# Feed-forward pieces beside attention: 64x128 tiles of the array in place of pairs of 64x64

## The chip, the cores and the metric

The kernel runs on one core of a Trainium2 chip. The metric is the device time of one execution in microseconds (us). The median of three runs of the kernel before is 318.04 us (316.34 to 318.82). The execution that was profiled took 318.09 us.

## The reference

Attention with a softmax whose denominator has one more term, for 8 batches, 12 heads, 448 positions and a head size of 64, and behind it a feed-forward layer in which the largest of three products is taken, for 8 x 448 = 3,584 tokens of 768 values:

```python
def _attn_ref(q, k, v):
    scale = 1.0 / np.sqrt(q.shape[-1])
    scores = scale * np.matmul(q, k.transpose(0, 1, 3, 2))
    m = np.max(scores, axis=-1, keepdims=True)
    e = np.exp(scores - m)
    attn = e / (np.sum(e, axis=-1, keepdims=True) + np.exp(-m) + 1e-09)
    return np.matmul(attn, v)                     # (8, 12, 448, 64)

def _moe_ref(x, w1, w2, w3, w_out):               # w1, w2, w3, w_out: 768 x 768
    h = np.maximum(np.maximum(x @ w1, x @ w2), x @ w3)
    return h @ w_out
```

`x` is the attention's output with the heads side by side. The inputs and the output are float32.

## The kernel before, in words

The matmuls take 16-bit operands and sum in float32. The twelve heads of a batch are worked in three groups of four, so there are 24 groups, and a group's operands lie as two row halves of 64 partitions (`half(0)`, `half(1)`) by two columns, `c` = 0 and 1.

**Attention.** One visit (`visit`, L307) makes the scores of one block of 64 keys of a group with four matmuls on 64 rows by 64 columns of the TensorE array, one in each corner (`score_tile`, L291 to L301, tile `stp`; `TILES` gives the four corners). ACT takes the exponential (L318), DVE sums the blocks (L328). Per group there is one set of four matmuls for the denominator (`den_group`) and seven sets of four for the product with `v` (`num_group`), both through `av_tiles` (L340 to L348, matmuls at L342); ACT makes the reciprocal (L362, L369) and DVE the product that gives `xT` (`norm_group`, L397).

**Feed-forward beside attention.** A piece is one 128 x 448 block of an up product (`up_piece`: batch, column block `fc`, which of the three weights) or one 128 x 384 block of the output (`out_piece`). Each contracts 768 values, in `NDC` = 6 blocks of 128 rows, into one PSUM bank.

**Three phases.** In the first (to some 71 us in the trace) pieces run as ordinary matmuls on 128 rows by 128 columns (L534, L557) between the 64x64 matmuls of attention. In the second (71.7 to 237.4 us) attention of groups 7 to 23 goes on, and pieces run as *half steps*, which is what the change touches. In the third there is no attention, and the rest of the feed-forward runs on 128 by 128 (L1034, L1236).

**Half steps.** `piece_parts` (L741) gives the width (`S` = 448 or `NW` = 384 columns) and two functions that slice weights and moving data. `half_step(r)` (L768) does one of a piece's six blocks on row half `r`: it has to write 128 output rows, and does so with two matmuls, `c` = 0 and 1, of 64 rows by 64 columns (L782), into the lower and the upper 64 partitions of the piece's bank. Both row halves work on different pieces, since both write whole banks: each takes a batch of three pieces in another order (`turns`). A piece is done by one half first and then by the other, which starts with `start` unset and adds to what lies in the bank; before that an empty instruction on PE waits until the first half's last matmuls have ended (`wait_for`, L758, on `p["last"]`). When the second half is through, DVE or ACT empties the bank (`up_piece`, L518 to L523; `out_piece`, L565 to L575).

**Order.** The whole program is written out by hand: each engine works its list in that order, with semaphores between engines. `step()` (L830) gives a half step to row half 0 and then one to row half 1. The loop at L970 walks through groups and the entries of `ORDER` (seven visits, the denominator, the product with `v`), and puts steps between them, as many as the planner's rates ask for (`steps_for`) or as are needed until a score bank should be free (`for_pair`, from booked costs of DVE and ACT in units of steps). So stretches of half steps and sets of attention matmuls alternate on PE.

Of the kernel before, what the change touches and what calls it, by code (L numbers as in the profile page):

```python
# [14 lines left out]
ts = bass.ts  # L15
# [7 lines left out]
def kernel(  # L23
# [11 lines left out]
    nc = tc.nc  # L35
# [4 lines left out]
    KC = 64  # L40
    NJ = S // KC
    NDC = DM // 128
# [50 lines left out]
    def ring_bank(name):  # L93
        ring[0] += 1
        pool = single_pools[ring[0] // 2 % 2]
        return pool.tile([128, 512], FP32, tag="bank1", name=name)
# [7 lines left out]
    def half(n):  # L104
        return slice(n * KC, n * KC + KC)
# [54 lines left out]
    for _ in range(WQ):  # L160
        for r in range(2):
            for c in range(2):
                nc.tensor.matmul(
                    out=warm[r][c * KC : c * KC + KC, 0:WN],
                    lhsT=ones16[r * KC : r * KC + KC],
                    rhs=warm16[r * KC : r * KC + KC],
                    start=True,
                    stop=True,
# [3 lines left out]
    w_sb = [cpool.tile([128, NDC, DFF], MMDT, name=f"w{i}") for i in range(4)]  # L172
# [324 lines left out]
    hT = {}  # L497
    outs = {}

    def new_h(b, fc, i):  # L500
        if b // 2 not in hT:
            hT[b // 2] = ht_pool.tile([128, NFC, 2 * S], MMDT, tag="hT", name="hT")
# [158 lines left out]
    start = """  # L661
# [79 lines left out]
    def piece_parts(f, a):  # L741
        if f is up_piece:
            b, fc, i = a
            new_h(b, fc, i)
            return (
                S,
                lambda k, r, c: w_sb[i][half(r), k, fc * 128 + c * KC : fc * 128 + c * KC + KC],
                lambda k, r: xT[b][half(r), k],
            )
        bp, t, nh = a  # L750
        return (
            NW,
            lambda k, r, c: hT[bp][half(r), k, t * 128 + c * KC : t * 128 + c * KC + KC],
            lambda k, r: wout_sb[half(r), k, ts(nh, NW)],
        )


    def wait_for(matmuls):  # L758
        nop = nc.tensor.nop()
        for mm in matmuls:  # L760
            tc.add_manual_dep(
                nop.ins,
                mm.ins.name,
                mybir.DependencyInfo(mybir.DependencyClass.Sync, mybir.DependencyReason.DATA),
                reason="both row halves write one bank",
            )

    def half_step(r):  # L768
        n, k = divmod(count[r], NDC)
        count[r] += 1  # L770
        p = flow[turns[r][n]]
        if k == 0 and "parts" not in p:
            p["parts"] = piece_parts(p["f"], p["a"])
            p["bank"] = ring_bank("piece")
            p["first"] = r
        elif k == 0:
            wait_for(p["last"])
        w, lhs, rhs = p["parts"]
        p["last"] = []
        for c in range(2):  # L780
            p["last"].append(
                nc.tensor.matmul(  # L782
                    out=p["bank"][half(c), 0:w],
                    lhsT=lhs(k, r, c),
                    rhs=rhs(k, r),
                    start=(r == p["first"] and k == 0),
                    stop=(r != p["first"] and k == NDC - 1),
                )
            )
        if r != p["first"] and k == NDC - 1:  # L790
            p["f"](*p["a"], bank=p["bank"], done=True)
            p["done"] = True
# [37 lines left out]
    def step():  # L830
        if count[0] == NDC * len(turns[0]) and (len(pieces) >= 3 or last_batch[0] and pieces):
            m = len(flow)
            now = pieces[:3]
            del pieces[:3]
            flow.extend({"f": f, "a": a} for f, a, w in now)
            for r in range(2):
                turns[r] += [m + x for x in ((0, 2, 1), (1, 0, 2))[r] if x < len(now)]
        before = sum(count)
        idle = not ready(0)
        if not idle:  # L840
            half_step(0)
        if (count[1] + LAG < count[0] or idle) and ready(1):
            half_step(1)
        steps[0] += 1
        do_late()
        return sum(count) > before
# [123 lines left out]
    for i in range(MID, NI + 1):  # L970
        for op, j, w in ORDER if i > MID else ORDER[4:]:
# [23 lines left out]
            if op == "N":  # L995
# [4 lines left out]
                t = max(steps[0] + 1, state[i - 1]["recip"])  # L1000
# [253 lines left out]
    def in_turn(*units):  # L1254
        return [u[slot] for slot in range(max(map(len, units))) for u in units if slot < len(u)]
# [20 lines left out]
    first = in_turn(*(up(2, f) for f in range(SOONER, 3)))  # L1276
# [64 lines left out]
```

## Time and profile before

| what | us |
| --- | --- |
| median of three runs | 318.04 (316.34 to 318.82) |
| the profiled execution | 318.09 |
| its span, first to last instruction | 316.3 |
| PE busy in the span | 301.6 (95%) |
| PE weight loads busy | 216.3 (68%) |
| DVE busy | 246.0 (78%) |
| ACT busy | 230.8 (73%) |
| L782, piece matmuls of 448 and of 384 columns, busy | 121.7 and 29.4 |

Busy time of PE counts a stretch with at least one matmul in flight. A matmul's record is longer than the time after which the next can start, so the distance between starts tells the pace, and the duration doesn't. In the profile, `64*64` ahead of a shape is the part of the array that an instruction takes, rows by columns. The granted TensorE clock is given as a share of full speed.

### The profile page before, as it was taken

What the parts mean: (1) busy time and instruction counts of PE and PEld (TensorE: products, weight loads), DVE (VectorE), ACT (ScalarE), POOL (GpSimd) and SP (SyncE); (2) the same over time, 40 slices, a digit from 0 to 9 for tenths busy, and PEclk for the clock granted to TensorE, in tenths of its full rate; (3) what the DMA queues carried; (4) which work ended last, traced back from release to release, by engine and by line L of the source; (5) the groups of instructions that cost most, each with busy time, mean ns of one, the idle gap of its engine ahead of it and who ended that gap; (6) DMA issues with size and microseconds to landing.
All of it is one profiled execution on the core that took longest, in us unless ns stands there. A gap on an engine that the chain in (4) does not pass through costs nothing.

```text
span 316.3 us, 11901 instructions
## 1 busy us (share of the span) xinstructions
PE 301.6 (95%) x5200; PEld 216.3 (68%) x5200; DVE 246.0 (78%) x453; ACT 230.8 (73%) x315; POOL 82.8 (26%) x137
## 2 busy tenths in 40 slices
PE   6779999999999999999999999999999999999992
PEld 6557777658999767777679867777765555556551
DVE  3546598999889787988877898877867994989652
ACT  1999859987888987888887889999844547451540
POOL 8654341220433333434423434110000000000220
PEclk9999999999999999999999999999999999999998
DMA  8999999699778999789999999970003000002676
GB/s 149 192 203 205 208 208 204 89 149 179 118 104 135 180 171 182 99 124 168 229 136 137 100 172 232 155 89 4 2 2 101 4 0 2 0 0 72 186 236 205
DMA packets 59348, 40.58 MB, mean 128 GB/s; under 512 B 32256, under 2 KB 56288, under 8 KB 59296
## 3 DMA queue, kind: packets, MB, share of 16 engines
q0 software_dynamic: 25104, 21.80, 47.4%
q1 hardware_dynamic: 33648, 17.21, 27.7%
q8 instruction: 40, 0.66, 0.9%
q10 hardware_dynamic: 544, 0.82, 0.9%
q14 instruction: 12, 0.10, 0.1%
HBM read 42.47 MB, written 11.01 MB: 169 GB/s over the span
## 4 chain that ended last, share of the span: by engine, by line
PE 83%; ACT 8%; DVE 3%; issue 3%; DMA 1%; DVEq 0%; ACTq 0%
PE piece L782 35%; PE bank_a L1034 11%; PE stp L294 9%; PE av L342 8%; PE bank_s L1034 8%; PE p_i L534 4%; ACT eTp L416 3%; PE bank_a L1236 2%; PE piece L534 2%; ACT eT L318 2%; PE den L342 1%; DMA first_k<-in_k_dram 1%; PE piece L557 1%; DVE eS L328 1%; ACT rb L460 1%
## 5 line engine op out<-in xcount | busy, mean ns | idle before, releaser
L318 ACT ACTIVATE eT<-stp 128x896 f16<-128x896 f32 x147 | 129.1, 921 | 21.3 <-PE stp L294 21.1
L782 PE MATMUL piece<-xT,w 64*64 64x448 f16 x1968 | 121.7, 350 | 0.4 <-DVE xT L397 0.3
L782 PEld LDWEIGHTS <-w 64*64 64x64 f16 x1968 | 79.3, 107 | 17.0 <-issue 1.6
L294 PE MATMUL stp<-qkT 64*64 64x448 f16 (+2 forms) x756 | 65.2, 334 | 3.4 <-issue 1.3
L328 DVE TENSOR_TENSOR eS<-eS,eT 128x896 f16<-128x896 f16 x105 | 65.0, 619 | 3.4 <-ACT eT L318 0.2
L523 DVE TENSOR_TENSOR hT<-hT,piece 128x448 f16<-128x448 f16 x52 | 32.2, 619 | 13.9 <-PE piece L782 8.8
L294 PEld LDWEIGHTS <-qkT 64*64 64x64 f16 x756 | 29.4, 105 | 18.5 <-issue 7.3
L342 PE MATMUL av<-eT,ld_v 64*64 64x448 f16 x588 | 32.9, 350 | 0.2
L342 PEld LDWEIGHTS <-ld_v 64*64 64x64 f16 x756 | 26.5, 107 | 7.0 <-issue 1.5
L397 DVE TENSOR_TENSOR xT<-av,rb 128x448 f16<-128x448 f32 x42 | 24.2, 619 | 8.7 <-PE av L342 7.3
L114 POOL DMA_DIRECT2D ld_v<-in_v_dram x28 | 16.7, 598 | 52.5 <-PE stp L294 31.8
L782 PE MATMUL piece<-w,hT 64*64 64x384 f16 x456 | 29.4, 323 | 0.1
L583 POOL DMA_DIRECT2D out_dram<-o x7 | 3.8, 536 | 93.7 <-DVE o L1164 92.1
L114 POOL DMA_DIRECT2D ld_k<-in_k_dram x26 | 15.4, 595 | 39.5 <-PE stp L294 35.1
L362 ACT ACTIVATE rb<-den 128x896 f32<-128x896 f32 x21 | 19.3, 917 | 8.4 <-PE den L342 8.2
L416 ACT ACTIVATE eTp<-stp 128x768 f16<-128x768 f32 (+3 forms) x24 | 18.2, 821 | 7.1 <-PE stp L294 7.0
L534 PEld LDWEIGHTS <-w 128*128 128x128 f16 x216 | 18.9, 98 | 5.3 <-issue 3.6
L1034 PEld LDWEIGHTS <-comb 128*128 128x128 f16 x132 | 12.9, 98 | 12.2 <-issue 0.4
L782 PEld LDWEIGHTS <-hT 64*64 64x64 f16 x456 | 18.6, 107 | 3.6 <-issue 0.3
L369 ACT ACTIVATE rb<-rb 128x896 f32<-128x896 f32 x21 | 20.0, 952 | 0.2
L534 PE MATMUL p_i<-xT,w 128*128 128x192 f16 (+1 forms) x156 | 16.4, 257 | 0.6 <-DVE xT L490 0.6
L114 POOL DMA_DIRECT2D ld_q<-in_q_dram x26 | 15.7, 617 | 1.1 <-issue 1.1
(103 smaller groups left out, 405.0 us busy)
## 6 DMA issues: line engine op xcount, KB each, us to landing
out_dram<-o_sb SPq DMA_DIRECT2D x28, 192.0 KB, 4.9
ld_v<-in_v_dram POOLq DMA_DIRECT2D x28, 112.0 KB, 4.3
ld_k<-in_k_dram POOLq DMA_DIRECT2D x26, 112.0 KB, 3.5
ld_q<-in_q_dram POOLq DMA_DIRECT2D x26, 112.0 KB, 4.9
out_dram<-o SPq DMA_DIRECT2D x14, 192.0 KB, 3.3
ld_q<-in_q_dram POOLq DMA_DIRECT2D x11, 224.0 KB, 9.7
ld_k<-in_k_dram POOLq DMA_DIRECT2D x10, 224.0 KB, 9.5
ld_v<-in_v_dram POOLq DMA_DIRECT2D x10, 224.0 KB, 9.0
```

What stands on the lines that cost most here:

```text
L114: return eng.dma_start(out=dst[half(hp)].rearrange("p s j d -> p s (j d)"), in_=rows_of(name, i)[half(hp)])
L294: mm = nc.tensor.matmul(out=out[half(c), r], lhsT=qkT[half(r), 0, j, h], rhs=qkT[half(r), 1, q0:q1, h], start=True, stop=True,)
L318: nc.scalar.activation(out=st["eT"][:, j], in_=stp[:, :, 0:S], func=AF.Exp, scale=scale, bias=-math.log(EDIV))
L328: nc.vector.tensor_tensor(out=st["eS"], in0=st["eT"][:, 0] if j == 1 else st["eS"], in1=st["eT"][:, j], op=ALU.add,)
L342: nc.tensor.matmul(out=outs[r][half(c)], lhsT=weights(r, c), rhs=moving(r, c), start=start, stop=stop,)
L369: nc.scalar.activation(out=st["rb"], in_=st["rb"], func=AF.Exp, bias=math.log(LAMBDA), scale=-1.0)
L397: nc.vector.tensor_tensor(out=xT[b][:, 2 * g + r, :], in0=banks[r][:, 0:S], in1=state[i]["rb"][:, r], op=ALU.mult)
L416: nc.scalar.activation(out=eT[:, j0 : j0 + n].rearrange("p j r q -> p r j q"), in_=stp[:, :, 0 : n * nq].rearrange("p r (j q) -> p r j q", ...
L523: nc.vector.tensor_tensor(out=dst, in0=dst, in1=p_i[:, 0:S], op=ALU.max)
L534: nc.tensor.matmul(out=p_i[:, ts(j, nq)], lhsT=w_sb[i][:, dc, ts(2 * fp + j, 128)], rhs=xT[b][:, dc, q0 * KC : q1 * KC], start=(dc == 0), ...
L782: nc.tensor.matmul(out=p["bank"][half(c), 0:w], lhsT=lhs(k, r, c), rhs=rhs(k, r), start=(r == p["first"] and k == 0), stop=(r != p["first" ...
L1034: nc.tensor.matmul(out=bank, lhsT=lhs(k), rhs=rhs(k), start=start and k == 0, stop=k == 2, skip_group_check=True,)
```

## The change

A half step issues one matmul on its 64 rows and all 128 columns, in place of two on 64 columns each. The slices of the weights lose their column index, the output is all 128 partitions of the bank, and `p["last"]` holds one matmul. The order of half steps, attention and all other work is the same, and so is what is computed.

```diff
@@ piece_parts
             return (
                 S,
-                lambda k, r, c: w_sb[i][half(r), k, fc * 128 + c * KC : fc * 128 + c * KC + KC],
+                lambda k, r: w_sb[i][half(r), k, ts(fc, 128)],
                 lambda k, r: xT[b][half(r), k],
             )
         bp, t, nh = a
         return (
             NW,
-            lambda k, r, c: hT[bp][half(r), k, t * 128 + c * KC : t * 128 + c * KC + KC],
+            lambda k, r: hT[bp][half(r), k, ts(t, 128)],
             lambda k, r: wout_sb[half(r), k, ts(nh, NW)],
         )
@@ half_step
         w, lhs, rhs = p["parts"]
-        p["last"] = []
-        for c in range(2):
-            p["last"].append(
-                nc.tensor.matmul(
-                    out=p["bank"][half(c), 0:w],
-                    lhsT=lhs(k, r, c),
-                    rhs=rhs(k, r),
-                    start=(r == p["first"] and k == 0),
-                    stop=(r != p["first"] and k == NDC - 1),
-                )
-            )
+        p["last"] = [
+            nc.tensor.matmul(
+                out=p["bank"][:, 0:w],
+                lhsT=lhs(k, r),
+                rhs=rhs(k, r),
+                start=(r == p["first"] and k == 0),
+                stop=(r != p["first"] and k == NDC - 1),
+            )
+        ]
```

## The prediction

> **What bounds the kernel now.** I read the page's busy shares and its chain of work first, then the busy time by stage, then the timeline of TensorE (PE) in three places. The profiled execution took 318.09 us with a span of 316.3; the three other runs have a median of 318.04 (316.34 to 318.82). All sums below are made against 318.1, and a difference under 1% (3.2 us) can hardly be told from no change on this kernel.
>
> From the page, the chain that ended last:
>
> ```profile
> PE 83%; ACT 8%; DVE 3%; issue 3%; DMA 1%; DVEq 0%; ACTq 0%
> PE piece L782 35%; PE bank_a L1034 11%; PE stp L294 9%; PE av L342 8%; PE bank_s L1034 8%; PE p_i L534 4%; ACT eTp L416 3%; PE bank_a L1236 2%; PE piece L534 2%; ACT eT L318 2%; PE den L342 1%; DMA first_k<-in_k_dram 1%; PE piece L557 1%; DVE eS L328 1%; ACT rb L460 1%
> ```
>
> The reader is to see that the end is set by PE and that the changed line, L782, is its largest single part. Busy time by stage (columns: us, then PE, weight loads, DVE, ACT, POOL, granted clock, DMA share, GB/s):
>
> ```profile
> 71.70:237.40 165.70, 165.25 (x3460) 128.80 (x3459) 137.96 (x255) 139.31 (x175) 47.55 (x80) 1.00 0.86 130
> ```
>
> All of L782 lies in this stage, and PE is busy in 165.25 of its 165.70 us while DVE and ACT have some 26 to 28 us free. What PE gains or loses here moves the end nearly one for one. The next question is whether PE waits inside that busy time, and the timeline answers it (columns: start, us from first start to last end, engine, line):
>
> ```profile
> 154.47 0.36 PE L294 MATMUL stp<-qkT 64*64 64x448 f16 x4
> 154.66 0.74 PE L782 MATMUL piece<-xT,w 64*64 64x448 f16 x12
> 155.23 0.36 PE L294 MATMUL stp<-qkT 64*64 64x448 f16 x4
> 155.42 1.49 PE L782 MATMUL piece<-xT,w 64*64 64x448 f16 x28
> 156.74 0.36 PE L342 MATMUL den<-eS,ones 64*64 64x448 f16 x4
> 156.93 0.36 PE L294 MATMUL stp<-qkT 64*64 64x448 f16 x4
> ```
>
> Read the starts. Four matmuls on four 64x64 corners go together, and the next four start 0.19 later (154.47 to 154.66; 12 pieces take 0.57, 28 take 1.32). The single records give 0.189, and 0.162 where 384 columns stream (18 matmuls of L557 in the start phase are spaced alike). Attention (`stp`, `av`, `den`) and pieces follow each other without any gap: all are 64x64. Counting by these paces, the stage needs 492 groups of 448 (1,968/4) x 0.189 = 93.0, 114 of 384 (456/4) x 0.162 = 18.5, and 259 attention groups (464 of L294 and 572 of L342 between the first and the last piece, over 4) x 0.189 = 49.0, together 160.5 us of its 165.7. So some 5 us are gaps, and the rest is streaming.
>
> **The change, part by part.** (1) 2,424 loads and 2,424 matmuls of 64x64 become 1,212 of each on 64 rows by 128 columns. A group of a step is now two matmuls, one per row half, that stream the same 448 or 384 columns. I put its pace at the old 0.189 and 0.162: the pace already is that of streaming, and 128*128 matmuls of 448 columns in the last stage have it too (six of L1034 in 1.14 us). The halved loads save nothing, as they lie under matmuls: in the stage the load queue is busy 128.8 of 165.7. No instruction of DVE, ACT, POOL or the DMA queues is added or moved; the wait between two row halves (`wait_for`) names one matmul in place of two, which end 0.003 us apart. Cost 0.
>
> (2) The order now alternates between two shapes of the array. Counted in the changed kernel's order, the pieces form 132 stretches between attention, from 2 to 40 matmuls long (the commonest, 6). Each is entered from 64x64, and 131 return to it; the last goes to 128*128, where a change of shape already stands. That is 263 new changes of shape. The stage of before has none, but the start phase, where pieces run on 128*128 beside 64x64 attention, has some forty:
>
> ```profile
> 58.59 0.39 PE L342 MATMUL den<-eS,ones 64*64 64x448 f16 x4
> 58.91 1.48 PE L534 MATMUL piece<-xT,w 128*128 128x256 f16 x12
> 60.23 1.14 PE L557 MATMUL piece<-w,hT 128*128 128x384 f16 x6
> 61.29 0.57 PE L294 MATMUL stp<-qkT 64*64 64x448 f16 x8
> 61.70 0.39 PE L228 MATMUL trT<-ident,ld_k 64*64 64x64 f16 x28
> ```
>
> Four `den` matmuls should free the array after 0.19, but the next start is 0.32 later; six matmuls of 384 columns take 0.98, but the next start is 1.06 later; and the first two `stp` groups take 0.41, not 0.38. In the single records a change costs 0.096 us over the streaming of the last matmul before it: 15 of 15 changes from 128*128 to 64x64 lie between 0.095 and 0.097, and of 17 the other way ten lie between 0.091 and 0.100, two at 0.12, and five wait for something else. Then the first group after it is longer, since its loads were not made ahead: by 0.026 into 64x64 (0.025 to 0.033), by 0.013 into 128*128 (0.007 to 0.015), by 0.027 into 128*64. And the four matmuls of a group start 0.003 apart, so the last of them ends 0.010 after the first, which only matters when all must be done.
>
> No row has 64x64 beside 64x128, where the rows stay and only the columns merge. The nearest is a change that keeps 128 rows and alters only the columns:
>
> ```profile
> 5.99 0.40 PE L273 MATMUL trT<-ident,k 128*128 128x128 f16 x4 [1.18 <-DVE k L266]
> 6.31 0.36 PE L223 MATMUL trT<-ident,ld_q 128*64 128x128 f16 x6
> ```
>
> Four matmuls of 128 columns stream for 0.22; the next shape starts 0.32 later, again 0.10 too late. So I take 0.096 for every change; the ends are 0 (below) and 0.100. For the first group in 64x128 I take the 128*128 row, 0.012, as it too loads 128 columns; the ends are 0.007 and 0.027.
>
> The Trainium skill, "TensorEngine Tiling (Array Packing)", section Key Properties, says that changing the tiling mode, not merely the tile, drains the TensorE, and lists 64x128 and 64x64 as separate modes. This case's trace agrees for every pair of shapes that it has, with 0.096 us; by the rule the unseen pair pays as well.
>
> (3) Sum. Into pieces: 0.096 + 0.010 + 0.012 = 0.118; back: 0.096 + 0.026 = 0.122; together 0.24 us per stretch, x 131.5 = +31.6. From it go 263 x 0.0024 = 0.6, the bit by which a pace of 0.189 exceeds pure streaming (448 columns in 0.187). (4) Row halves: today one half may run ahead of the other where a 384-column piece faces a 448-column one, and makes up for it later; with a change of shape both must be done. Summing the busier half of each of the 132 stretches by the paces gives 112.6 against 111.5 for either half as a whole: +1.0. (5) The 5 us of gaps: PE's waits there are on `xT` and `eS` from DVE and on score banks. Slower PE work between them gives DVE and ACT some 18% more time, so part must go; with no way to see how much, I take 2.1 off (ends 0 and 4.2). The last stage has the same instructions and starts later by the whole sum. 318.1 + 31.6 - 0.6 + 1.0 - 2.1 = **348.0 us**, +9.4%.
>
> **The rivals.** *The change of shape is free* because both shapes keep the split into 64 rows, and only that split needs a drain. For it: no row shows this pair. Against: 5.99 to 6.31 keeps the rows and pays. Then nothing is added, the streaming pace stays, and the time is 318.1, no change; it decides if a change costs under 0.012 us (3.2/263). Below that the time could only fall by removing gaps, which fewer instructions don't do. Chance 0.09, of which 0.02 for faster. *In part:* the drain is shorter in this pair, or more of the gaps is absorbed: at half the price, 0.12 per stretch, 318.1 + 15.8 + 1.0 - 2.1 = 333. Chance 0.05. *The two row halves don't run together in 64x128*: each group then takes its streaming twice, + 93.0 + 18.5 = 111.5, 348 + 111.5 = 460. For it: no row shows two such matmuls at once; against: the halves do run together in 64x64 and drift apart freely there. Chance 0.03.
>
> *Loads are exposed.* Weight loads of 128*128 lie under matmuls on the same rows today:
>
> ```profile
> 48.70 1.15 PE L534 MATMUL piece<-xT,w 128*128 128x192 f16 x12 [0.43 <-ACT eT L318]
> 49.68 1.15 PE L534 MATMUL p_i<-xT,w 128*128 128x192 f16 x12
> ```
>
> Twelve start in 0.98, 0.082 each, while a load alone takes 0.098 (page, L534 PEld). Were each half's load exposed in 64x128, 606 groups x 0.098 = +59, so 407. Chance 0.01. This rival is a rule of the Trainium skill, "TensorE: Matmul & The Clock Gate", section The mechanism: a load overlaps matmuls in flight only when its row group differs. The rows just shown speak against it.
>
> **How the numbers follow.** Forecast 0.82; free 0.09; in part 0.05; serial 0.03; exposed loads 0.01. The forecast's own ends: all prices low, 263 x 0.091 + 131 x 0.025 + 132 x 0.007 + 1.3 (the 0.010) - 0.6 + 1.0 - 4.2 = +25.6, or +21.4 without the two first-group terms, 339; high, 263 x 0.100 + 131 x 0.033 + 132 x 0.027 + 1.3 - 0.6 + 1.0 = +35.9, 354. The range 339 to 354 holds most of the 0.82, and the cases left out stand at 0.18, so it isn't stretched to them. Faster by over 1%: 0.02. Within 1%: 0.07. Slower by over 1%: 0.91.
>
> **What would show it.** In the changed profile: L780 with 1,212 matmuls of 64*128, its groups 0.189 apart inside a stretch (serial halves: 0.378); starts of `stp` 0.28 behind the start of the last piece matmul, and 0.21 to the group after; the stage 71.7 to 237.4 longer by some 30 us with PE still nearly always busy; the first 71 us and the last 79 unchanged; DVE and ACT busy for the same time. A start of `stp` 0.19 after it would refute the price; gaps at changes that are there while the stage is short would mean that more gaps were absorbed than I allow.

## The result, and the profile after

The changed kernel takes 344.06 us (median of six runs, 343.68 to 344.37), the kernel before 317.81 in the runs beside it. The ratio is 1.0811, with a 95% interval from 1.0781 to 1.0842: slower by 8.1%, 26 us. The forecast was 348.0 in a range from 339 to 354. The profiled execution of the changed kernel took 344.13 us with a span of 342.4 (before 318.09 and 316.3).

The busy time by stage of the changed kernel (columns: us, then PE, weight loads, DVE, ACT, POOL, granted clock, DMA share, GB/s):

```profile
0.00:71.00 71.00, 63.37 (x1323) 47.43 (x1324) 49.09 (x97) 56.20 (x74) 31.55 (x50) 1.00 1.10 179
71.70:263.50 191.80, 191.74 (x2247) 77.51 (x2244) 138.83 (x255) 142.40 (x174) 47.73 (x80) 1.00 0.76 111
263.50:342.40 78.90, 72.69 (x419) 40.36 (x417) 58.33 (x101) 34.94 (x67) 3.76 (x7) 0.98 0.29 81
```

All of the difference lies in the second stage: 191.8 us where it was 165.7. The first piece of that stage starts 0.4 us earlier than before (71.29 us, before 71.68), the last stage takes 78.9 as before, and DVE has kept its busy time in the second stage (138.8, before 138.0). ACT is busy there for 142.4, before 139.3; that difference was not followed. PE is still marked busy almost throughout, 191.74 of 191.80: a change of shape doesn't show as idle time, because a matmul's record (0.35 us for 448 columns) reaches 0.16 us beyond the point at which the next could start (0.19). The loads tell more. Here are the groups of waits of the load queue (PEld) in the second stage, in us in total, times, and the longest:

```profile
PEld L294 <- issue: 31.7, 91, 0.4
PEld L780 <- issue: 29.8, 120, 0.4
PEld L342 <- issue: 5.8, 16, 0.4
```

At 91 scores, 120 pieces and 16 other places of attention the load queue stood for some 0.3 us, and `issue` says that the profile shows nothing it waited for. Before, the three lines held far less:

```profile
PEld L782 <- issue: 1.9, 6, 0.5
PEld L342 <- issue: 1.6, 5, 0.5
PEld L294 <- issue: 0.8, 4, 0.2
```

The loads of a new shape don't start while the matmuls of the old one stream: in the single records the first load at each change starts within 0.005 us of the first matmul of the new shape. The timeline shows what that does to the matmuls (start, us from first start to last end, engine, line):

```profile
155.06 0.65 PE L780 MATMUL piece<-w,hT 64*128 64x384 f16 x6
155.64 0.38 PE L294 MATMUL stp<-qkT 64*64 64x448 f16 x4
155.96 0.34 PE L780 MATMUL piece<-w,hT 64*128 64x384 f16 x2
156.22 0.38 PE L294 MATMUL stp<-qkT 64*64 64x448 f16 x4
156.54 0.99 PE L780 MATMUL piece<-w,hT 64*128 64x384 f16 x10
157.45 0.38 PE L294 MATMUL stp<-qkT 64*64 64x448 f16 x4
```

Read the starts again. The six matmuls of 384 columns at 155.06, two at a time, stream for 3 x 0.162 = 0.49, and the scores start 0.58 after the first of them; the scores stream for 0.19, and the next piece starts 0.32 later. The stretch at 155.96 is a single step: it streams for 0.16 us, and the two changes beside it add 0.13 (0.32 less 0.19, on the way in) and 0.10 (0.26 less 0.16, on the way back).

### The profile page after: what moved, and what is told of

The parts are those of the page before. It is cut to its first block, busy times and chain, and to the rows that moved or that the text cites. A ratio compares the mean times of both kernels' runs of the same rounds, so it can differ in the third digit from the quotient of the medians.

```text
span 342.4 us, 9478 instructions
## 1 busy us (share of the span) xinstructions
PE 328.2 (96%) x3988; PEld 165.5 (48%) x3988; DVE 246.9 (72%) x453; ACT 234.2 (68%) x315; POOL 83.0 (24%) x137
## 4 chain that ended last, share of the span: by engine, by line
PE 83%; ACT 7%; DMA 5%; issue 2%; DVE 2%; ACTq 0%; DVEq 0%
PE piece L780 37%; PE stp L294 12%; PE bank_a L1032 10%; PE av L342 8%; PE bank_s L1032 8%; DMA ld_v<-in_v_dram 3%; ACT eTp L416 3%; PE bank_a L1234 2%; PE den L342 2%; PE p_i L534 2%; PE piece L534 2%; DMA first_k<-in_k_dram 1%; ACT eT L318 1%; PE piece L557 1%; ACT rb L460 1%
## 5 line engine op out<-in xcount | busy, mean ns | idle before, releaser
L318 ACT ACTIVATE eT<-stp 128x896 f16<-128x896 f32 x147 | 131.6, 916 | 38.3 <-PE stp L294 37.2
L780 PE MATMUL piece<-xT,w 64*128 64x448 f16 x984 | 118.7, 351 | 0.4 <-DVE xT L397 0.3
L780 PEld LDWEIGHTS <-w 64*128 64x128 f16 x984 | 42.9, 94 | 51.9 <-issue 25.1
L294 PE MATMUL stp<-qkT 64*64 64x448 f16 (+2 forms) x756 | 60.9, 344 | 3.6 <-issue 1.2
L523 DVE TENSOR_TENSOR hT<-hT,piece 128x448 f16<-128x448 f16 x52 | 32.2, 619 | 25.1 <-PE piece L780 21.7
L294 PEld LDWEIGHTS <-qkT 64*64 64x64 f16 x756 | 20.8, 104 | 42.5 <-issue 38.2
L342 PE MATMUL av<-eT,ld_v 64*64 64x448 f16 x588 | 31.8, 352 | 0.0
L780 PE MATMUL piece<-w,hT 64*128 64x384 f16 x228 | 28.6, 325 | 0.0
L342 PEld LDWEIGHTS <-ld_v 64*64 64x64 f16 x756 | 20.0, 106 | 14.3 <-issue 3.8
L1032 PEld LDWEIGHTS <-comb 128*128 128x128 f16 x132 | 12.9, 98 | 12.2 <-issue 0.4
L780 PEld LDWEIGHTS <-hT 64*128 64x128 f16 x228 | 11.6, 94 | 10.1 <-issue 5.1
## 6 DMA issues: line engine op xcount, KB each, us to landing
out_dram<-o_sb SPq DMA_DIRECT2D x28, 192.0 KB, 4.5
out_dram<-o SPq DMA_DIRECT2D x14, 192.0 KB, 3.1
```

The costliest lines, as they stand in the source:

```text
L294: mm = nc.tensor.matmul(out=out[half(c), r], lhsT=qkT[half(r), 0, j, h], rhs=qkT[half(r), 1, q0:q1, h], start=True, stop=True,)
L318: nc.scalar.activation(out=st["eT"][:, j], in_=stp[:, :, 0:S], func=AF.Exp, scale=scale, bias=-math.log(EDIV))
L342: nc.tensor.matmul(out=outs[r][half(c)], lhsT=weights(r, c), rhs=moving(r, c), start=start, stop=stop,)
L523: nc.vector.tensor_tensor(out=dst, in0=dst, in1=p_i[:, 0:S], op=ALU.max)
L780: nc.tensor.matmul(out=p["bank"][:, 0:w], lhsT=lhs(k, r), rhs=rhs(k, r), start=(r == p["first"] and k == 0), stop=(r != p["first"] and k = ...
L1032: nc.tensor.matmul(out=bank, lhsT=lhs(k), rhs=rhs(k), start=start and k == 0, stop=k == 2, skip_group_check=True,)
```

## Experiments

**1. Is it the change of shape, or the wide matmul?** In this run of the changed kernel attention, too, goes on 64x128 in the second stage, so that nothing alternates. The core of the edit (the products with `v` and the denominators likewise):

```diff
 def score_tile(qkT, out, j, q0, q1):
+    if beside[0]:                    # second stage
+        for r in range(2):
+            mm = nc.tensor.matmul(
+                out=out[:, r],
+                lhsT=qkT[half(r), 0, j],
+                rhs=qkT[half(r), 1, q0:q1, half(0)],
+                start=True, stop=True,
+            )
+        return mm
     for r, c in TILES:
```

> Of the changed kernel: the pieces stay on 64x128, and in the second stage attention goes on 64x128 too, so that the stage has no change of shape left. Per row half, scores, denominators and products with v are one matmul with 128 columns of weights in place of two with 64; the moving data of the first column half serves both. So the second column half of attention is not computed (its results are wrong), while each group still streams 448 columns on both row halves for 0.189 us, and all work of ACT, DVE and the DMA queues stays. Theory (each change of shape costs about 0.12 us with its longer first group): all of the loss goes, 318 us (316 to 320). Rival (64x128 matmuls or their loads are slower in themselves): the loss stays or grows, 344 us or more.

Measured: 316.31 us (315.73 to 318.72) beside 318.54 for the kernel before, ratio 0.9919 (0.9885 to 0.9953). The loss is gone. From the first piece's start to the last piece's its trace has 163.8 us, where the kernel before has 165.5. Its timeline has the wide matmuls of pieces and attention one behind the other:

```profile
99.72 0.73 PE L800 MATMUL piece<-xT,w 64*128 64x448 f16 x5
100.17 0.46 PE L295 MATMUL stp<-qkT 64*128 64x448 f16 x2
100.36 1.03 PE L800 MATMUL piece<-xT,w 64*128 64x448 f16 x8
101.12 0.46 PE L295 MATMUL stp<-qkT 64*128 64x448 f16 x2
101.31 1.41 PE L800 MATMUL piece<-xT,w 64*128 64x448 f16 x12
```

100.17 to 100.36 is 0.19 again, and eight piece matmuls take 0.76, four times 0.19. So the wide matmul and its load are as fast as a pair of narrow ones, and the two row halves do run together in this shape. That it comes out 0.8% below the kernel before was not followed up; attention issues half as many instructions there, and half of its results are not computed.

**2. Many changes, few wide matmuls.** Only the first step of each stretch is wide. `wide()` decides whether a half step issues one matmul or a pair, and `fresh` is set by every set of attention matmuls:

```diff
+def wide():
+    return fresh[0]
...
+            for c in ((None,) if wide() else (0, 1))
...
+        fresh[0] = fresh[0] and sum(count) == before      # at the end of step()
```

> Of the changed kernel: only the first step of each of the 132 stretches goes on 64x128, the others on pairs of 64x64 as before. 263 wide matmuls in place of 1,212, but 264 changes of shape, one more than in the changed kernel. Theory: as slow as the changed kernel, 344 us (342 to 347). Rival of slower wide matmuls: 263/1,212 of 26.2 = +5.7, 323.5 us.

Measured: 346.76 us (344.66 to 347.19), ratio 1.0848 (1.0777 to 1.0920). With 263 of 1,212 wide matmuls it is as slow as the changed kernel (its interval contains the whole of that one's), and 23 us from what its rival gives. What counts is how often the shape changes.

**3. Half of the changes.** The same switch, with the condition that attention is at groups 7 to 14:

```diff
+def wide():
+    return now_at[0] < 15
```

> Of the changed kernel: pieces go on 64x128 while attention is at groups 7 to 14, and on pairs of 64x64 from group 15 on. 62 stretches and 534 of the 1,212 wide matmuls are left, 124 changes of shape in place of 263. Theory: 62 x 0.236 = 14.6 us of price, plus 0.5 for the row halves, less the gaps of that half of the stage, about 2.5: +12.6, 331 us (328 to 333). Rival of slower wide matmuls: 534/1,212 of 26.2 = +11.5, 329.5; this run alone doesn't part the two, but both need the loss to be proportional, where a loss made at one place (a late score bank, the start of the stage) would give 318 or 344.

Measured: 330.84 us (329.91 to 331.28), ratio 1.0359 (1.0296 to 1.0422). 124 changes of 263 make 12.3 us of some 26: the loss comes in proportion, as both readings expected.

**4. Another pair of shapes.** A piece's matmuls go on the whole array, 128 rows by 128 columns, at the place of the half steps of row half 0; those of row half 1 issue nothing:

```diff
...
+        if r == 0:
+            nc.tensor.matmul(
+                out=p["bank"][:, 0:w],
+                lhsT=lhs(k), rhs=rhs(k),             # all 128 rows
+                start=(k == 0), stop=(k == NDC - 1),
+            )
...
```

> Of the changed kernel: a piece's half steps on row half 0 become matmuls on all 128 rows and 128 columns, and those on row half 1 issue nothing; what is computed is the same, at the same 0.189 and 0.162 per block. The 132 stretches and 263 changes of shape stay, now between 64x64 and 128x128; the row halves of a piece need not wait for each other. Theory (what costs is any change of shape, whichever parts of the array merge): 344 us (341 to 347), with the row halves' 1.0 us saved at most. Rival (the pair 64x64 and 64x128 is a special one, dearer or cheaper than a change of rows and columns): under 340 or over 348.

Measured: 342.98 us (342.63 to 343.60), ratio 1.0745 (1.0682 to 1.0809). Columns alone or rows and columns, the loss is nearly the same. Read from the starts of the single records, going back to 64x64 costs 0.0965 us from 128x128 and 0.0933 from 64x128 (means of 131); going out costs 0.112 in both, with the longer first group of an attention stretch in it where the stretch has only one group.

**5. Fewer changes by another order.** Two blocks of scores are made per visit, so that the pieces form 56 stretches. It was run with wide pieces and, as its companion, with the pairs of 64x64:

```diff
...
-                for_pair()
-                mm = visit([(i, j)])
...
+                two = [j, j + 1] if j < 6 and (i, j) != (MID, 3) else [j]
+                for_pair(max(pair_free) if len(two) == 2 else 0.0)
+                mm = visit([(i, j) for j in two])
...
```

> Of the changed kernel: two blocks of scores at a time (blocks 0 and 1, 2 and 3, 4 and 5 of a group are made in one visit, when both score banks are free), so that the same pieces on 64x128 form 56 stretches in place of 132, with 112 changes of shape between 64x64 and 64x128. Theory: the price falls to 56 x 0.236 + 0.5 = 13.7 us, but ACT, which now gets two blocks at once and then none until both banks are empty, makes PE wait in new places. Against the same order on 64x64 pieces (its companion run) it is 13.7 us slower at most, and less by what its price hides of that run's gaps: 6 to 13.7. Rival of slower wide matmuls: the wide matmuls are all there, so 26 us slower than the companion.

> The kernel before with the same order by pairs of blocks: no change of shape between 64x64 and 64x128, so that what it loses is the order alone: ACT idle until two banks are refilled, some 0.4 us per pair, in part hidden since ACT is busy 139 of 166 us. 318 to 335 us; no theory is parted by it alone.

Measured: 380.65 us wide (ratio 1.1953, 1.1900 to 1.2005) and 367.37 with pairs of 64x64 (1.1534, 1.1484 to 1.1584). The difference is 13.3 us, at the price of 56 stretches (13.7) and half of the 26 that all of the wide matmuls would carry with them. The order itself was misjudged: it costs 49 us, far over the 0 to 17 that were expected. In the second stage of the companion PE is busy for 157.8 of 181.0 us:

```profile
70.00:251.00 181.00, 157.82 (x3236) 118.16 (x3228) 119.81 (x219) 120.62 (x155) 46.42 (x78) 1.00 0.77 115
```

With gaps of 23 us there, one might have thought that they would swallow part of the price. The difference leaves little room for that: from the first piece's start to the last piece's the two traces have 193.7 and 181.2 us, and behind the last piece 114.0 and 113.1. Why the gaps didn't swallow more was not followed.

Where the 49 us of the order itself lie, the trace of the companion shows. From the first piece to the last it takes 15.7 us more than the kernel before (181.2, before 165.5), and there the pieces are used up: the last one starts at 252.0 us, while attention goes on until 284.7. In the kernel before, pieces outlast attention. So for 32.5 us PE has attention alone, waits on ACT and DVE, and is busy for 20.0 us, at a mean granted clock of 0.69:

```profile
252.20:284.70 32.50, 20.00 (x216) 8.59 (x208) 17.79 (x30) 24.64 (x29) 1.18 (x2) 0.69 0.14 22
```

The expectation saw only ACT's idle time at each pair; it didn't see that this order spends the same pieces on fewer groups, which leaves none beside the last of the attention.

**6. How much of the stage's gaps does added work swallow?** The price seen in the trace is more than the loss (below). So PE work without any change of shape was added to the kernel before, at places where the changed kernel has changes:

```diff
-            mm = score_tile(st["qkT"], stp[:, :, 0:S], j, 0, NJ)
+            for _ in range(1 + beside[0]):
+                mm = score_tile(st["qkT"], stp[:, :, 0:S], j, 0, NJ)
```

> The kernel before, with each of the 116 sets of four score matmuls of the second stage issued twice in a row into the same bank (the same result; the second set starts the sum anew). That adds 116 x 0.189 = 21.9 us of PE work at places where the changed kernel has a change of shape, without any change of shape. Question: how much of the stage's 5 us of gaps does added PE work swallow? If all of it, as the trace of the changed kernel suggests: +17, ratio 1.053, 335 us. If the 2.1 us that the prediction took: +19.8, ratio 1.062, 338. If none: +21.9, ratio 1.069, 340.

Measured: 336.57 us, ratio 1.0566 (1.0505 to 1.0627): 18.0 us for 21.9 us of work, with an interval from 16.1 to 20.0. So between 1.9 and 5.8 us vanish. That nothing is swallowed lies outside of this interval; the 5 of the stage and the 2.1 that the prediction took both lie within. Which waits vanished, the trace can't show: the profiled execution took 341.68 us and has two long waits of its own (0.62 us before 211.11 and 2.69 before 220.04).

**7. Can the kernel before be rid of changes that it has?** Its first stage transposes q and k of groups 1 to 3 on 128x64, between matmuls of 64x64:

```diff
-        tiled = i > NG
+        tiled = i > 0
```

> The kernel before, whose first stage transposes q and k of groups 1 to 3 on 128x64: these go on 64x64 like those of later groups, same result. 6 changes of shape of the first stage vanish, 3 of them into 128x64 and 3 back. Theory: 6 x 0.096 + 6 x 0.027 = 0.7 us, and the transposes themselves take half of 0.78 us each time, 1.1 in all; at most 1.8 us faster, 316, as far as PE and not ACT or a load sets the end there; no change (318) if ACT does.

Measured: 324.66 us (321.72 to 327.54), ratio 1.0128 (1.0074 to 1.0182): slower by 1.3%, where up to 1.8 us of gain was expected. Six changes less, and the time is lost elsewhere. First the tenths of PE's granted clock over the span, in 40 slices (9 is 90% or more), then the busy time of three short windows:

```profile
PEclk9769999999999999999999999999999999999999
```

```profile
9.00:11.00 2.00, 0.98 (x57) 0.65 (x43) 1.57 (x3) 1.34 (x3) 0.69 (x2) 1.00 1.23 187
11.00:13.00 2.00, 0.95 (x50) 0.66 (x44) 0.05 (x1) 1.51 (x2) 0.66 (x1) 0.62 1.24 196
13.00:16.00 3.00, 3.00 (x98) 2.84 (x94) 1.68 (x4) 2.19 (x4) 2.02 (x3) 0.50 1.39 203
```

From 9 to 13 us PE is busy for less than half of the time. The clock falls to half at 11.5 us and stays there until 21.7. In the kernel before it is 1.00 in all three windows, with 1.14 and 2.00 us of PE work in the first two. The timeline names the waits:

```profile
10.11 0.27 PE L294 MATMUL stp<-qkT 64*64 64x192 f16 x1 [0.76 <-DVE qkT L252]
10.64 0.52 PE L294 MATMUL stp<-qkT 64*64 64x192 f16 x15 [0.26 <-DVE qkT L252]
11.91 0.60 PE L228 MATMUL trT<-ident,ld_k 64*64 64x64 f16 x28 [0.75 <-DMA ld_k<-in_k_dram]
12.81 0.59 PE L228 MATMUL trT<-ident,ld_q 64*64 64x64 f16 x28 [0.30 <-DMA ld_q<-in_q_dram]
```

The last two wait for the loads of group 2. In both kernels the loads were issued at the same times, but here they came later. POOL, whose next issue waits for the same `ld_k`, shows by how much; in the kernel before this issue began at 11.42:

```profile
12.15 0.66 POOL L188 DMA_DIRECT2D w<-in_moe_w_dram  x1 [2.46 <-DMA ld_k<-in_k_dram]
```

So a load that was 0.7 us late, PE idle around it, and then some 10 us at half clock are what the profiled execution shows of the loss up to the second stage: its first piece starts 4.7 us later than before (76.34, before 71.68), of the 7.2 by which the span is longer (323.5, before 316.3). The other 2.5 were not followed. Why the load was late, and whether the other executions lost their time in the same place, stays open; the price of six changes is too small to be seen beside it.

## Why the prediction held, step by step

**What bounds the kernel.** The reading that the stage is all streaming and that PE's gain or loss there moves the end nearly one for one held: the last stage starts 26.1 us later (263.57, before 237.43), and the span is 26.1 longer (342.4, before 316.3).

**(1) The pace of wide matmuls at the old 0.189 and 0.162, cost 0:** held. Inside stretches the groups of the changed kernel follow at 0.189, and run 1, where only the pace is left, loses nothing. With it fall the rivals of serial halves (460) and of exposed loads (407). The rule of the Trainium skill, "TensorE: Matmul & The Clock Gate", section The mechanism, that a load overlaps matmuls in flight only where its row group differs, is not what this chip does here: both row halves stream all the time, and loads of 0.094 us on the same rows fit beneath them at 0.189 per group.

**(2) The price of a change, 0.096 from other pairs of shapes:** held for the pair that no row had shown. In the single records 131 returns to 64x64 cost 0.093 us on average. Of the 132 entries into 64x128, 94 follow a stretch of attention that is a single group and cost 0.118 to 0.119, 37 follow a longer one and cost 0.094 to 0.095, and one waits for something else. The 0.024 between them is the longer first group, which in a stretch of one is also the last. The first group in 64x128 is longer by 0.011 over the pace (0.200, where the next ones take 0.189), close to the 128*128 row that was taken, and not the 0.027 of the other end. The rival that a change is free because the rows stay is refuted by the same records. The rule of the Trainium skill, "TensorEngine Tiling (Array Packing)", section Key Properties, is that any change of the mode drains the array; this trace agrees, now with 0.093 and 0.095 us beside it for this pair.

**(3) and (4) The sum of the prices, 32.0 us with the row halves:** nearly. The records give 14.7 us for entries and 12.2 for returns, 1.4 for first groups in 64x128 and 0.9 for first groups of the attention stretches of more than one group. With the 1.3 for the spread of four starts, the -0.6 and the +1.0 of the row halves as predicted, it is 30.9, 1.1 less than forecast; some 0.4 of that is the return, which was priced 0.003 too high, and the rest lies in the first groups and in the entries.

**(5) The gaps, 2.1 us taken off: this term was mis-sized.** From the first piece's start to the last piece's, the stage takes 165.5 us before and 192.0 after, 26.5 more. Against prices of 30.9, some 4.4 us of gaps have gone, of the 5 that there were. The load queue shows part of it. Its line of waits for `xT`, first in the kernel before and then in the changed one:

```profile
PEld L294 <- DVE xT L397: 3.0, 11, 0.4
PEld L294 <- DVE xT L397: 1.3, 4, 0.4
```

That is 1.7 us; that these waits now lie in time that a change of shape takes anyway is the likely reading, and the other waits were not traced one by one. Run 6 gives 1.9 to 5.8 us for a smaller amount of added work (21.9 us), which parts neither the 2.1 nor the 4.4 from it. The 2.1 was the middle between two ends, 0 and 4.2, taken for want of any row; the records put the term at the far end. Gaps and prices together explain 3.4 of the 3.9 us between 348.0 and the profiled execution's 344.1; the 0.4 by which the first piece starts earlier, in a stage that the change doesn't touch, is most of the remainder.

**What would show it:** the stage longer by some 30 us with PE nearly always busy (26), scores 0.28 behind the start of the last piece matmul (0.280 from the mean of the returns), the first 71 us and the last 79 unchanged (71 and 78.9), and no other engine with more instructions. The row-half term was not measured by itself. Run 4, where no row half can hold the other up, is 1.1 us faster than the changed kernel's 344.06, about that term, and in the traces its stage is 1.4 us shorter from the first piece's start to the last piece's (190.6, changed kernel 192.0); but the two were timed on different occasions and the intervals of their ratios overlap.

## What to carry to other kernels

Before halving the number of matmuls by a wider tile of the array, look at what stands beside them on PE: where two shapes alternate, every change cost some 0.12 us here with the longer group behind it, whether columns alone or rows and columns merged, and a busy PE didn't show it. Count the changes in the instruction order and multiply. Waits of the same engine in that stage can take part of it off, as they did for some 4 of 31 us here, but not always: in run 5 the gaps of 23 us took hardly any. Stay in one shape where two kinds of work are interleaved finely; both shapes stream at the same pace.

## What the hardware showed that was not expected

The granted clock fell to half in run 7 without any long pause: the waits of PE between 9.4 and 12.8 us are 0.3 to 0.8 us each, with a busy share of half over 4 us, and the clock, which falls there, stayed at half through 3 us in which PE was busy all the time. The companion of run 5 shows the like where attention is alone: after 9.4 us in which PE was busy for 4.37, with no wait over 1.6, the clock was at half from 261.4 to 268.2 us, and again from 271.6 to 285.3, at 1.00 in between.

And changes of columns alone and of rows and columns cost the same within 0.004 us (returns to 64x64 of 0.0933 and 0.0965), although only in one of them do the tiles of a row half stay where they are. Rows alone change where the first stage of the kernel before goes from 128*64 to 64x64; the two of those four changes that wait for nothing else cost 0.096 and 0.097.
